# One PSUM ring, merged score halves and DMA transposes in a windowed-attention plus SwiGLU kernel

## The chip, the cores and the metric

The kernel runs on one core of one Trainium2 chip. The metric is the device time of one execution in microseconds (us). Executions are repeated in rounds beside the kernel before on the same chip; e1 to e4, e5 to e8 and e9 to e11 below ran on three different chips, so between these groups the ratios and the traces are compared, not the medians. Engines are named as in the profile: PE (matmuls), PEld (weight loads, which overlap PE: 249.1 and 133.4 us busy in a span of 272.5 before the change), DVE (vector), ACT (scalar), POOL (GpSimd, which also issues the input loads) and SP (which issues outputs and, after the change, transposes). The profile infers from semaphore events who waited for whom.

## The reference, cut to what matters

```python
# q, k, v: (4 batches, 8 heads, 768 positions, 64), float32; n_sink 4, window 128
scores = q @ k.T / 8                      # kept: the first 4 keys, and the last 128 positions
a = softmax(where(keep, scores, -1e9)) @ v
x = a as (3072 tokens, 512)
xn = x / sqrt(mean(x * x) + 1e-6) * rms_g
out = (silu(xn @ w_gate) * (xn @ w_val)) @ w_out      # 512 -> 1536 -> 512
```

The 3072 tokens are 24 blocks of 128 (g = 0 to 23, six to a batch; t is the place in the batch). The feed-forward part (FFN) takes them in six groups of four blocks (G = 0 to 5): gate and value matmuls (pg, pvl), then output matmuls (po).

## The kernel before

The order of PE's instructions is written by hand: the FFN is a list of parts of four to eight matmuls, and the attention of later blocks is woven in between. The attention of a block is a step of four quarters ("slots"). The order on DVE, ACT and POOL is the scheduler's.

```python
def step(g):                                  # before
    slots[0].append(lambda: unit_s(g, 0))     # scores + exponential + mask, half 0 of the heads
    slots[2].append(lambda: unit_s(g, 1))     # half 1
    ...                                       # sink keys (t == 1), sink scores (t in 2, 4)
    slots[1].append(lambda: unit_av(g - 1, 0))   # attention value of the block BEFORE
    slots[3].append(lambda: unit_av(g - 1, 1))
    slots[0].append(lambda: unit_x(g - 3))       # PE transposes of x, copied to xnt by ACT
    slots[2 if t != 5 else 1].append(lambda: unit_t(g + 2))   # PE transposes of q, k; qkT copied by ACT

def unit_sink(b):                             # keys of the four sinks, block-diagonal
    ks = sink.tile([P, HP * KSW], BF16, name="ksk")           # pool "sink" has 2 buffers
    nc.vector.memset(ks, 0.0)
    for hi in range(2):
        nc.vector.tensor_copy(out=ksv[pr, :, ...], in_=QKT[b][pr, 1, :, 0:NS])   # reads qkT of t = 0
```

Names of tiles in the profile: pqk, qkT are the transposed q and k in PSUM and after the copy; pT the scores, et their masked exponentials, ksk the sink keys, pss, esk the sink scores and their exponentials; pv the attention value, x the attention output, sq its squares, xr the normalized x; pxt, xnt its transpose in PSUM and after the copy; hT the product that enters po.

In any step the attention value uses scores of the step before, and x is transposed two steps after that. PSUM is split by use: 4 banks for everything that is one bank wide, 2 for score tiles (pT), 2 for the attention value (pv).

The softmax here doesn't subtract the row's maximum and nothing guards it: scores larger than these inputs give would overflow.

## Time and profile before

Median 275.3 us at the prediction (273.4 to 275.5, three runs), 274.4 us with a fourth run.

From the page of the kernel before, the busy us of each engine (share of the span, instructions), and the busy tenths of the DMA engines in 40 slices of the span:

```profile
PE 249.1 (91%) x1864; PEld 133.4 (49%) x1864; DVE 186.6 (68%) x493; ACT 156.3 (57%) x297; POOL 96.4 (35%) x129
...
DMA  9999999999999930120000220000130000210012
```

The table of windows of the same kernel. The columns are bounds and length in us, then busy us with instructions for PE, PEld, DVE, ACT and POOL, the granted PE clock, the time of the DMA packets as a multiple of the 16 engines' time (packets overlap, so it can exceed 1) and GB/s:

```profile
60.00:80.00 20.00, 18.72 (x180) 10.49 (x178) 16.88 (x58) 18.46 (x36) 19.19 (x22) 1.00 2.40 167
80.00:100.00 20.00, 20.00 (x159) 10.16 (x158) 18.42 (x51) 13.42 (x27) 11.42 (x14) 1.00 1.90 140
120.00:140.00 20.00, 19.93 (x158) 10.04 (x157) 14.92 (x38) 13.65 (x27) 4.29 (x8) 1.00 0.04 15
```

PE is the limit from 60 us on. Until about 95 us the DMA engines are full (9 tenths busy or more in each of the first 14 slices; loads of q, k, v in small pieces: 75440 of the run's 84230 packets are under 512 bytes). What a matmul costs PE is read here from when the next one starts, not from its listed length: the four of pg below are listed with 1.03 us, and the next matmul starts 0.86 us after the first of them, at 132.78 us. Timeline of PE in the kernel before (start, length, what, how many):

```profile
130.18 1.03 PE L417 MATMUL pvl<-xnt,wv 128*128 128x512 bf16 x4
131.14 0.39 PE L279 MATMUL pT<-qkT 64*128 64x256 bf16 x4
131.46 0.40 PE L201 MATMUL pqk<-ident,qs 128*128 128x128 bf16 x4
131.70 0.39 PE L201 MATMUL pqk<-ident,ks 128*128 128x128 bf16 x4
131.92 1.03 PE L417 MATMUL pg<-xnt,wg 128*128 128x512 bf16 x4
```

Four 512-column matmuls take 4 x 216 = 0.864 us, yet pT starts 0.96 us after pvl: entering the scores cost about 0.095 us. The four score matmuls (64 rows each) start in pairs, the two of a pair 3 ns apart; where eight stand in a row (the changed kernel at 64.10 us) a pair starts every 109 ns, so four are worth 4 x 54.5 ns = 0.22 us. Yet 0.32 us pass before pqk: leaving cost 0.10 us. The eight 128-column transposes from 131.46 to 131.92 take 56 ns each from start to start, and are listed with 0.22 to 0.23 us. So this trace puts a round trip into the scores and back at about 0.2 us; why it takes that is not shown.

### The profile page before, as it was taken

What the parts mean: (1) busy time and instruction counts of PE and PEld (TensorE: products, weight loads), DVE (VectorE), ACT (ScalarE), POOL (GpSimd) and SP (SyncE); (2) the same over time, 40 slices, a digit from 0 to 9 for tenths busy, and PEclk for the clock granted to TensorE, in tenths of its full rate; (3) what the DMA queues carried; (4) which work ended last, traced back from release to release, by engine and by line L of the source; (5) the groups of instructions that cost most, each with busy time, mean ns of one, the idle gap of its engine ahead of it and who ended that gap; (6) DMA issues with size and microseconds to landing.
All of it is one profiled execution on the core that took longest, in us unless ns stands there. A gap on an engine that the chain in (4) does not pass through costs nothing.

```text
span 272.5 us, 4924 instructions
## 1 busy us (share of the span) xinstructions
PE 249.1 (91%) x1864; PEld 133.4 (49%) x1864; DVE 186.6 (68%) x493; ACT 156.3 (57%) x297; POOL 96.4 (35%) x129
## 2 busy tenths in 40 slices
PE   1637978998999999999999999899999999999994
PEld 1325766874554544455444454444544454444441
DVE  2591888799788999437798458698337997078710
ACT  2554847769887666557557557558556353333311
POOL 8996369199997601223112001112322000000000
PEclk9999999999999999999999999999999999999998
DMA  9999999999999930120000220000130000210012
GB/s 58 132 175 186 203 160 182 167 155 149 174 199 183 155 14 0 70 88 0 2 1 2 77 77 2 0 2 0 43 113 2 0 2 19 96 41 0 0 68 86
DMA packets 84230, 21.01 MB, mean 77 GB/s; under 512 B 75440, under 2 KB 81072, under 8 KB 84208
## 3 DMA queue, kind: packets, MB, share of 16 engines
q0 software_dynamic: 80752, 14.42, 67.7%
q1 hardware_dynamic: 3456, 6.29, 6.2%
q8 instruction: 14, 0.23, 0.3%
q14 instruction: 8, 0.07, 0.1%
HBM read 28.57 MB, written 6.29 MB: 128 GB/s over the span
## 4 chain that ended last, share of the span: by engine, by line
PE 70%; DVE 8%; DMA 8%; POOL 6%; ACT 5%; issue 1%; POOLq 0%; ACTq 0%; DVEq 0%
PE po L458 22%; PE pg L417 18%; PE pvl L417 18%; DMA ks<-in_k_dram 5%; PE pT L279 4%; DMA wg<-in_moe_w_gate_dram 3%; PE pqk L201 3%; ACT et L286 2%; PE pxt L399 2%; DVE hT L443 2%; POOL ks L90 2%; PE pv L333 1%; ACT qkT L225 1%; POOL qs L90 1%; POOL v_98 L103 1%
## 5 line engine op out<-in xcount | busy, mean ns | idle before, releaser
L417 PE MATMUL pg<-xnt,wg 128*128 128x512 bf16 (+1 forms) x336 | 74.9, 352 | 2.9 <-ACT xnt L403 1.5
L417 PE MATMUL pvl<-xnt,wv 128*128 128x512 bf16 (+1 forms) x336 | 74.1, 349 | 0.0
L458 PE MATMUL po<-wo,hT 128*128 128x512 bf16 x288 | 66.8, 379 | 0.0
L430 ACT ACTIVATE th<-pg 128x512 bf16<-128x512 f32 x72 | 42.8, 595 | 37.8 <-PE pg L417 37.6
L286 ACT ACTIVATE et<-pT 128x1024 bf16<-128x1024 f32 (+1 forms) x48 | 45.2, 946 | 8.9 <-PE pT L279 8.8
L301 POOL TENSOR_SCALAR_AFFINE_SELECT et<-et 128x512 bf16<-128x512 bf16 x20 | 13.2, 660 | 99.6 <-ACT et L286 99.6
L417 PEld LDWEIGHTS <-wg 128*128 128x128 bf16 x336 | 31.3, 99 | 28.1 <-issue 3.1
L417 PEld LDWEIGHTS <-wv 128*128 128x128 bf16 x336 | 31.2, 98 | 25.4 <-issue 0.6
L458 PEld LDWEIGHTS <-hT 128*128 128x128 bf16 x288 | 26.7, 98 | 27.6
L465 ACT ACTIVATE osb<-po 128x512 f32<-128x512 f32 x24 | 14.4, 598 | 24.4 <-PE po L458 19.0
L90 POOL DMA_DIRECT2D ks<-in_k_dram x24 | 21.6, 901 | 6.9 <-DMA wo<-in_moe_w_out_dram 3.5
L225 ACT COPY qkT<-pqk 128x1024 bf16<-128x1024 bf16 x21 | 21.2, 1007 | 5.1 <-PE pqk L201 5.1
L90 POOL DMA_DIRECT2D qs<-in_q_dram x24 | 21.7, 904 | 6.6 <-DMA wo<-in_moe_w_out_dram 2.6
L342 DVE RECIPROCAL rden<-pv 128x4 f32<-128x4 f32 x48 | 8.5, 176 | 19.6 <-PE pv L333 19.5
L279 PE MATMUL pT<-qkT 64*128 64x256 bf16 (+1 forms) x192 | 18.9, 276 | 2.5 <-ACT qkT L225 1.7
L299 DVE TENSOR_TENSOR et<-et,masks 128x1024 bf16<-128x1024 bf16 (+1 forms) x28 | 18.1, 647 | 1.4 <-ACT et L286 1.1
L201 PE MATMUL pqk<-ident,qs 128*128 128x128 bf16 x96 | 10.3, 236 | 7.1 <-DMA qs<-in_q_dram 6.9
L403 ACT COPY xnt<-pxt 128x512 bf16<-128x512 bf16 x24 | 14.0, 581 | 4.6 <-PE pxt L399 4.5
L279 PEld LDWEIGHTS <-qkT 64*128 64x128 bf16 x192 | 6.2, 95 | 18.5 <-issue 17.9
L333 PEld LDWEIGHTS <-et 128*128 128x128 bf16 x192 | 13.5, 100 | 3.2 <-DVE et L299 1.2
L328 PEld LDWEIGHTS <-et 128*128 128x128 bf16 x160 | 12.9, 99 | 3.8 <-DVE x_319 L343 0.7
L399 PE MATMUL pxt<-ident,xr 128*128 128x128 bf16 x96 | 9.9, 229 | 4.2 <-DVE r L374 2.6
(303 smaller groups left out, 341.7 us busy)
## 6 DMA issues: line engine op xcount, KB each, us to landing
out_dram<-osb SPq DMA_DIRECT2D x24, 256.0 KB, 2.0
qs<-in_q_dram POOLq DMA_DIRECT2D x24, 128.0 KB, 7.0
ks<-in_k_dram POOLq DMA_DIRECT2D x24, 128.0 KB, 6.7
wg<-in_moe_w_gate_dram POOLq DMA_DIRECT2D x4, 384.0 KB, 10.0
wv<-in_moe_w_val_dram POOLq DMA_DIRECT2D x4, 384.0 KB, 11.2
wo<-in_moe_w_out_dram POOLq DMA_DIRECT2D x2, 768.0 KB, 11.0
v_98<-in_v_dram POOLq DMA_DIRECT2D x6, 128.0 KB, 7.9
v_100<-in_v_dram POOLq DMA_DIRECT2D x6, 128.0 KB, 7.6
```

Of the source, the lines that this page charges most:

```text
L90: nc.gpsimd.dma_start(out=tl, in_=src[b, :, t * P:(t + 1) * P, :].rearrange("h t d -> t h d"),)
L201: nc.tensor.transpose(out=ps[:, c0 + hp * P:c0 + (hp + 1) * P], in_=src[:, 2 * hp:2 * hp + 2, :], identity=ident,)
L225: nc.scalar.copy(out=QKT[b].rearrange("p i h s -> p (i h) s")[:, :, t * P:(t + 1) * P], in_=ps.rearrange("p (x c) -> p x c", c=P),)
L279: nc.tensor.matmul(out=pT[:, hi, j * 256:j * 256 + w], lhsT=QKT[b][pr, 1, hp, t * P:(t + 1) * P], rhs=QKT[b][pr, 0, hp, t * P:t * P + w], ...
L286: nc.scalar.activation(out=et[:, :, 0:nq, :].rearrange("p x n c -> p x (n c)"), in_=pT.rearrange("p i (j c) -> p (i j) c", c=256)[:, :, 0: ...
L299: nc.vector.tensor_tensor(out=ev, in0=ev, in1=mv, op=ALU.mult)
L333: nc.tensor.matmul(out=dest, lhsT=E[(g, u)][:, x, 0, :], rhs=V16[b][:, t, h, :], start=(t == 0), stop=True, skip_group_check=True,)
L399: nc.tensor.transpose(out=ps[:, kt * P:(kt + 1) * P], in_=xr[:, kt * P:(kt + 1) * P], identity=ident,)
L417: nc.tensor.matmul(out=ps[:, i * n:(i + 1) * n], lhsT=w_sb[:, kt, ft * P:(ft + 1) * P], rhs=XNT[G][:, kt, cols], start=(kt == 0), stop=(kt ...
L430: nc.scalar.activation(out=st["th"], in_=st["pg"], func=ACT.Tanh, scale=0.5)
L458: nc.tensor.matmul(out=st["po"], lhsT=HT[(G, ft // 2)][:, ft % 2, tb * P:(tb + 1) * P], rhs=wo[:, ft, :], start=(ft == 0), stop=(ft == FTN ...
L465: nc.scalar.mul(osb, st["po"], 0.5)
```

## The change

It makes PSUM one ring of eight single banks, runs both score halves of a block back to back, puts a block's attention value into the same step as its scores, moves late transposes from PE to DMA (x from block 8, q and k from block 12), shortens the reciprocal square root by one DVE instruction, and broadcasts the RMS weight by an f32 matmul in place of a broadcast load. It also rearranges the order by hand of the first blocks, which the cut leaves out. Cut to its core:

```diff
-    POOL_MASK_FROM = 2            # by batch
-    MANUAL = {mybir.EngineType.PE}
+    POOL_MASK_FROM = 12           # by block: the same blocks
+    X_DMA_FROM = 8
+    QK_DMA_FROM = 12
+    MANUAL = {mybir.EngineType.PE, mybir.EngineType.SP}
+    ring = ctx.enter_context(tc.tile_pool(name="ring", bufs=8, space=bass.MemoryType.PSUM))
+    def unit_gb():
+        nc.tensor.matmul(out=ps, lhsT=ones, rhs=grow, start=True, stop=True)     # f32
+    def unit_td(g):
+        for i, src in ((1, KS_.pop(g)), (0, QS.pop(g))):
+            nc.sync.dma_start_transpose(out=qkT[:, i, :, t * P:(t + 1) * P], in_=...)
...   # unit_s: both halves, one exponential a bank; unit_av: both halves, one Square a block
     def step(g):
-            slots[0].append(lambda: unit_s(g, 0))
-            slots[2].append(lambda: unit_s(g, 1))
+            slots[0].append(lambda: unit_s(g))
+            slots[2].append(lambda: unit_av(g))
-            slots[1].append(lambda: unit_av(g - 1, 0))
-            slots[3].append(lambda: unit_av(g - 1, 1))
-            slots[0].append(lambda: unit_x(g - 3))
+        if g - 2 < X_DMA_FROM:
+            slots[0].append(lambda: unit_x(g - 2))
+        if X_DMA_FROM <= g < NB:
+            slots[3].append(lambda: unit_x(g))
-            slots[2 if t != 5 else 1].append(lambda: unit_t(g + 2))
+        if g + 2 < QK_DMA_FROM:
+            slots[3 if t != 5 else 1].append(lambda: unit_t(g + 2))
+        if QK_DMA_FROM <= g + 4 < NB:
+            slots[1].append(lambda: unit_td(g + 4))
...   # one pass of sink scores for four blocks from batch 2 on
     with tc.manual_schedule(engines=MANUAL):
         unit_t1(0, 0)
         unit_t1(0, 1)
+        unit_gb()
         unit_t1(1, 0)
```

## The prediction

> **What bounds it.** The page gives PE 91% of the 272.5 us span, DVE 68%, ACT 57%. From 60 us on the table of windows shows PE at 19-20 us of every 20, at full clock. Start-to-start times of matmuls in the timeline: 216 ns for 512 columns, 109 ns for 256, 56 ns for a 128-column transpose, 30 ns for an attention-value matmul, 54 ns for a score matmul of 256 columns (pairs overlap). Summed: about 231 us. The other 41 us: 5 before the first matmul, 17 of gaps up to 30 us (loads, then the rsqrt chain), 5 from 30 to 60 us, 11 after 60 us, 4 of tail. Of the 11 about 8 are switches: some 95 ns to enter and 100 ns to leave each run of 64-row score matmuls.
>
> **What goes.** (1) PE transposes: x from block 8 (16 x 4), q, k from block 12 (12 x 8): 160 x 56 ns = 9.0 us, all where PE limits. (2) Score halves in one run: 24 fewer switches of 0.2 us, 4.8 us, of which I count 3.8 where PE limits. (3) One sink-score pass for two, no gb broadcast on the POOL queue, the 1.5 us gap at 170 us: about 1 us. ACT loses 16 x 0.58 (xnt), 12 x 1.01 (qkT), about 0.45 per block for the Square; it gains 48 fixed parts of about 0.17 us, the exponential being split by bank (585 ns for 512 columns, 1018 for 1024). DVE loses one 0.2 us operation per block. ACT and DVE aren't the limit after 100 us.
>
> **What it adds.** (a) Scores and their attention-value product stand in the same step. The chain is four exponentials (2.4 us) plus mask (0.69 on DVE, about 1.25 per half on POOL). Late, four FFN parts (3.46 us) lie between; I count 1 us. In the first output stage (60-75 us) only 1 to 1.5 us lie between, and the next scores wait for a 1.0 us qkT copy: I estimate a step of 6 us against 4.7 in the trace, three steps, 3.5 us lost. (b) The f32 gb matmul[...] stands ahead of the q1 transposes in the ramp; with longer exponentials I estimate 1 us. (c) 40 DMA transposes of 128 KB. [...] q, k are issued three steps (about 25 us) ahead of use, x about two; even 3 us each should hide.
>
> **Sum.** 9 + 3.8 + 1 - 1 - 3.5 - 1 = 8.3 us off. The constants look tuned, so my penalties may be too high: I add 2.5 us. 275.3 - 10.8 = 264.5 us; 8 in 10 within 258 to 271. Chances: faster by over 2% 0.80, within 0.17, slower 0.03.
>
> **What would show it.** PE instructions 1864 to about 1680; no xnt or qkT copies on ACT after about 100 us; one entry to pT per block; late stages shorter by about 2 us per four blocks. (a): waits of pv for et, by DVE in 60-75 us, by POOL later. (b): first pg later than 21.9 us. (c): no wait of pg for xnt, or of pT for qkT, on a DMA.
>
> **What would make it wrong.** DMA transposes of several us each, serial on one queue and starving the loads (DMA engines over 90% busy to 95 us); the eight-bank ring making pg wait for an old score bank whose exponential queues on ACT; the same-step chain stalling PE in every block (1 us each would cancel the gain); or the early stall not appearing.

Two passages are cut where marked. The 3 us of (c) are an assumption, not a reading.

## The result, and the profile after

The changed kernel took 271.36 us (median of four, 270.8 to 272.2) against 274.44 us: a ratio of 0.988, 95% interval 0.984 to 0.992. Ratios here are the mean time of one kernel's fast runs over that of the other's fast runs of the same rounds, so not quite the ratio of the medians quoted.

The prediction, 264.5 us within 258 to 271, was too low. The time lies just above the range, and in the class (within 2%) that had been given 0.17.

Where the time went is seen by cutting both traces at the same points of PE's work. The table is worked out from start times in the timelines of the two profiled runs (us):

| stage | before | after | difference |
|---|---|---|---|
| start to first gate matmul (ramp) | 21.93 | 23.22 | +1.3 |
| first gate matmul to first po of G 0 | 38.41 | 39.62 | +1.2 |
| first po of G 0 to first gate matmul of G 1 | 20.02 | 28.73 | **+8.7** |
| first gate matmul of G 1 to last matmul | 188.12 | 173.70 | **-14.4** |
| last matmul to the end | 4.02 | 4.45 | +0.4 |
| span | 272.5 | 269.7 | -2.8 |

One caution on these traces. At the first gate matmul PE still runs at half its clock in every one of them (256-column matmuls start 216 ns apart, later 109 ns). The clock records packed with the traces tell when it became full, and this differs: at 25 to 27 us in the kernel before, e2, e5, e7, e9 and e10 (25.4, 26.9, 26.4, 26.4, 25.7, 25.0), at 30 to 32 us in after, e1, e3, e4, e6, e8 and e11 (31.1, 31.2, 31.2, 32.0, 30.6, 30.0, 30.5). The column of the granted clock in the tables of windows reads 1.00 there all the same, since it counts nothing before the first record. The timelines of after and then of e2, which has the same PE work in this stage:

```profile
28.01 1.89 PE L438 MATMUL pvl<-xnt,wv 128*128 128x256 bf16 x8
...
27.57 1.05 PE L438 MATMUL pvl<-xnt,wv 128*128 128x256 bf16 x8
```

The stage from the first gate matmul to the first po took 39.62 us in after and 38.01 in e2, so the late clock is worth about 1.6 us, and more than covers the +1.2 of the table. What decides when it comes is not shown. Runs of one kernel seem to take both: in e1, e6 and e8, profiled with the late clock, the profiled run belongs to a slower group of the fast runs (e1: 267.2 and 267.7 us against 265.6 and 265.7), and in e2, e7, e9 and e10, profiled with the early clock, to the faster. So where two traces differ in this, 1.6 us of their difference are not counted as the edit's.

The late stages gained a little more than the 12.8 us that the prediction's terms amount to there (9 + 3.8 + 1 - 1); part of it, about 0.6 us, is work that the change moved to earlier stages. One early stage, the output matmuls of group 0, gave back more than half. The page of the changed kernel shows PE's share fall, and a dip in the clock granted to PE (tenths, in 40 slices):

```profile
PE 240.3 (89%) x1698; PEld 128.5 (48%) x1698; DVE 179.0 (66%) x471; ACT 135.5 (50%) x267; POOL 96.9 (36%) x128
...
PEclk9999999999997999999999999999999999999999
```

The table of windows of the changed kernel places the loss:

```profile
60.00:80.00 20.00, 13.89 (x141) 8.55 (x139) 13.41 (x42) 11.54 (x24) 17.87 (x21) 1.00 2.53 153
80.00:100.00 20.00, 17.47 (x130) 9.38 (x130) 14.11 (x42) 13.38 (x28) 10.51 (x12) 0.91 2.04 171
120.00:140.00 20.00, 20.00 (x134) 9.64 (x132) 12.02 (x35) 10.74 (x21) 5.25 (x8) 1.00 0.44 102
```

From 60 to 80 us PE fell from 18.7 to 13.9 busy us, and DVE and ACT fell with it. All compute engines idling more at once suggests that they wait for one another or for a DMA, not that one has more to do. In the next window the clock was 0.91. The list of waits of the changed kernel (who waited for whom: us in all, times, longest), PE's from 60 to 95 us, DVE's over the span:

```profile
PE pT L303 <- ACT qkT L237: 5.6, 4, 4.2
PE pv L361 <- DVE et L325: 1.9, 3, 0.9
PE pv L345 <- ACT esk L285: 1.1, 1, 1.1
...
DVE ksk L256 <- DMA qkT<-ks: 3.6, 1, 3.6
```

The last line had not been foreseen at all. Timeline of the changed kernel from 70 to 82 us (in brackets, the idle time before and what ended it):

```profile
70.59 1.37 SPq L245 DMA_TRANSPOSE qkT<-ks  x1
...
76.16 0.39 PE L218 MATMUL pqk<-ident,ks 128*128 128x128 bf16 x4
...
76.38 1.03 PE L482 MATMUL po<-wo,hT 128*128 128x512 bf16 x4
...
78.31 0.35 DVE L256 COPY ksk<-qkT 64x16 bf16<-64x16 bf16 x2 [3.64 <-DMA qkT<-ks]
78.69 0.18 DVE L368 RECIPROCAL rden<-pv 128x4 f32<-128x4 f32 x1
...
79.97 0.63 ACT L376 ACTIVATE sq<-x 128x512 bf16<-128x512 bf16 x1 [3.24 <-DVE x L369]
...
80.60 0.99 ACT L237 COPY qkT<-pqk 128x1024 bf16<-128x1024 bf16 x1
...
81.64 0.61 PE L303 MATMUL pT<-qkT 64*128 64x256 bf16 x8 [4.23 <-ACT qkT L237]
...
82.49 1.91 PE L482 MATMUL po<-wo,hT 128*128 128x512 bf16 x4
```

Read it from the bottom. PE waits 4.2 us for a qkT copy on ACT, though the last transposes that it copies started at 76.2 us and took 0.4 us. ACT has a Square ahead of that copy, and the Square waits 3.2 us for x from DVE. DVE has two tiny copies, 0.17 us each, ahead of the reciprocal for x. They build the sink keys of batch 2, which are first needed at block 14, several steps later. The scheduler put them here, at block 8, and they wait for the DMA transpose of block 12, issued at 70.6 us and landed at 78.3 us. The last line shows the after-effect: four output matmuls took 1.91 us from the first start to the end, where 76.38 us shows 1.03. They started 427 ns apart in place of 216, so PE was at half its clock until about 85.7 us (the clock record: 3.4 us from 82.3 us on). PE had hardly a gap in it, so by estimate half of it, 1.7 us, was lost on top of the wait.

Two things are read from the traces here. DVE did not run the reciprocal ahead of the two copies: the attention-value matmuls before it had ended by 75.2 us, but it started at 78.69, after the copies and the 3.6 us of idle time before them. And a gap of 4.2 us on PE (to 81.6 us) was followed by the half clock from 82.3 us on; in e4 the half clock came with a gap of 2.3 us (64.2 to 66.5 us, half clock from 66.1 to 69.5), while gaps of 1.2 to 1.9 us in the kernel before, e4, e6 and e11 were not followed by it. The traces show no more than that of what takes the clock down.

The DMA transposes themselves, in the list of DMA issues of the changed kernel, from 60 to 100 us and then from 120 to 220 us (the last number is the median time from issue to landing, us):

```profile
qkT<-ks SPq DMA_TRANSPOSE x3, 7.7
qkT<-qs SPq DMA_TRANSPOSE x3, 8.2
xnt<-xr SPq DMA_TRANSPOSE x2, 7.2
...
xnt<-xr SPq DMA_TRANSPOSE x11, 2.4
qkT<-ks SPq DMA_TRANSPOSE x7, 2.4
qkT<-qs SPq DMA_TRANSPOSE x7, 2.5
```

The first list is of 60 to 100 us, beside the saturated loads (DMA at 9 tenths or more throughout): there a transpose took 7 to 8 us at the median to land; from 120 to 220 us it took 2.4 to 2.5. The prediction had no measured time for one, and its assumption of 3 us was less than half of what they took beside the loads. 39 of the 40 issues also held SP's queue for 1.2 to 1.4 us, one for 1.9. The list of waits shows none of PE for a DMA transpose, since PE's first readers come later. What had been overlooked was a reader on DVE.

### The profile page after: what moved, and what is told of

Same layout as the page of the kernel before. It is cut to its first block, busy times and chain, and to the rows that moved or that the text cites. A ratio compares the mean times of both kernels' runs of the same rounds, so it can differ in the third digit from the quotient of the medians.

```text
span 269.7 us, 4662 instructions
## 1 busy us (share of the span) xinstructions
PE 240.3 (89%) x1698; PEld 128.5 (48%) x1698; DVE 179.0 (66%) x471; ACT 135.5 (50%) x267; POOL 96.9 (36%) x128
## 4 chain that ended last, share of the span: by engine, by line
PE 80%; DVE 7%; ACT 6%; DMA 4%; issue 1%; POOL 0%; ACTq 0%; POOLq 0%
PE pg L438 22%; PE pvl L438 22%; PE po L482 21%; PE pT L303 5%; DMA qkT<-ks 3%; PE pv L361 2%; PE pqk L218 2%; DVE et L325 2%; ACT qkT L237 2%; DMA ks<-in_k_dram 2%; PE pv L356 2%; PE pv L345 1%; DVE x L369 1%; PE pss L279 1%; ACT et L312 1%
## 5 line engine op out<-in xcount | busy, mean ns | idle before, releaser
L459 DVE SCALAR_TENSOR_TENSOR p<-th,pg 128x512 bf16<-128x512 bf16 x72 | 49.1, 682 | 32.3 <-ACT th L451 31.8
L312 ACT ACTIVATE et<-pT 128x512 bf16<-128x512 f32 (+1 forms) x96 | 46.4, 568 | 13.1 <-PE pT L303 13.0
L467 DVE TENSOR_TENSOR hT<-p,pvl 128x512 bf16<-128x512 bf16 x72 | 49.3, 685 | 3.4
L488 ACT ACTIVATE osb<-po 128x512 f32<-128x512 f32 x24 | 14.4, 601 | 30.9 <-PE po L482 26.9
L98 POOL DMA_DIRECT2D qs<-in_q_dram x24 | 21.5, 894 | 7.2 <-DMA wo<-in_moe_w_out_dram 2.1
L376 ACT ACTIVATE sq<-x 128x512 bf16<-128x512 bf16 x24 | 15.1, 628 | 16.4 <-DVE x L369 16.4
L303 PE MATMUL pT<-qkT 64*128 64x256 bf16 (+1 forms) x192 | 15.4, 279 | 8.5 <-ACT qkT L237 6.7
L111 POOL DMA_DIRECT2D v<-in_v_dram x24 | 21.3, 888 | 4.4 <-DMA qs<-in_q_dram 1.4
L369 DVE TENSOR_TENSOR x<-pv,rden 128x256 bf16<-128x256 f32 x48 | 19.8, 420 | 0.6
L361 PE MATMUL pv<-v,et 128*128 128x65 bf16 x192 | 17.3, 200 | 3.1 <-DVE et L325 3.1
L404 DVE SCALAR_TENSOR_TENSOR xr<-x,r,gb 128x512 bf16<-128x512 bf16 x24 | 19.1, 798 | 0.6
L303 PEld LDWEIGHTS <-qkT 64*128 64x128 bf16 x192 | 7.9, 96 | 17.9 <-issue 17.2
```

The costliest lines, as they stand in the source:

```text
L98: nc.gpsimd.dma_start(out=tl, in_=src[b, :, t * P:(t + 1) * P, :].rearrange("h t d -> t h d"),)
L111: nc.gpsimd.dma_start(out=V16[b][:, t, :, 0:D], in_=v[b, :, t * P:(t + 1) * P, :].rearrange("h t d -> t h d"),)
L303: nc.tensor.matmul(out=pT[(u, hi)][:, j * 256:j * 256 + w], lhsT=QKT[b][pr, 1, hp, t * P:(t + 1) * P], rhs=QKT[b][pr, 0, hp, t * P:t * P + w],
L312: nc.scalar.activation(out=et[:, 2 * hi:2 * hi + 2, 0:nq, :].rearrange("p x n c -> p x (n c)"), in_=pT[(u, hi)].rearrange("p (j c) -> p j ...
L361: nc.tensor.matmul(out=dest, lhsT=E[(g, u)][:, x, 0, :], rhs=V16[b][:, t, h, :], start=(t == 0), stop=True, skip_group_check=True,)
L369: nc.vector.tensor_tensor(out=x16[:, 4 * u:4 * u + 4, :], in0=pvv[:, :, 0:D], in1=rden.unsqueeze(2).to_broadcast((P, 4, D)), op=ALU.mult,)
```

## The experiments

e1 to e4 are the changed kernel with one edit each. e5 to e10 keep the edit of e1, and e11 is e5 without it. All results were correct. Times are medians; ratios are to the kernel before of the same rounds.

### e1: the hoisted copies kept back

```diff
-        ks = sink.tile([P, HP * KSW], BF16, name="ksk")
+        ks = sink.tile([P, HP * KSW], BF16, name="ksk", bufs=1)
```

With one buffer, the copies of batch 2 need the sink scores of batch 1 to be done, so they cannot be hoisted past block 10.

> The changed kernel with one edit: the block-diagonal sink keys (ksk) get one buffer in place of two, so the copies for batch 2 can't be placed on DVE before block 10's sink scores have been read; they then come long after the q, k transpose of block 12 has landed. Theory A (head of line): in the changed kernel these two copies stand on DVE ahead of block 8's reciprocal and wait 3.6 us for the DMA transpose; DVE, ACT's qkT copy and PE stand still in turn (4.2 us before the scores at 81.6 us) and the clock throttles for a while (matmuls at 427 ns). Expected: no DVE wait of ksk on a DMA, the first output stage 28.7 -> about 22.5 us, 271.4 -> about 265.5 us. Rival B (same-step chain of exponential, mask and attention value sets the length of the steps): the next wait takes over, at most 2 us won. Rival C (the transposes crowd the saturated DMA engines and the loads come late): nothing won.

Measured: 266.43 us, ratio 0.970 (0.965 to 0.975). The wait of ksk for a DMA is gone, the first output stage took 24.94 us in place of 28.73, all later stages stayed as they were (173.69 us), and the mean granted clock is 1.0. The table of windows of e1:

```profile
60.00:80.00 20.00, 15.60 (x158) 9.58 (x156) 14.86 (x48) 14.25 (x29) 18.39 (x22) 1.00 2.20 150
80.00:100.00 20.00, 18.27 (x147) 9.55 (x146) 16.16 (x45) 11.77 (x25) 11.00 (x13) 1.00 1.93 169
```

PE got back about 2.5 us over the two windows and the full clock, but not the 38.7 us of before. Its waits from 60 to 95 us in e1:

```profile
PE pv L361 <- DVE et L325: 2.8, 5, 0.9
PE pT L303 <- ACT qkT L237: 2.3, 4, 0.9
PE pv L345 <- ACT esk L285: 1.1, 1, 1.1
```

Theory A was right about the place, too high about the size: 3.8 us won in this stage where about 6 had been expected. PE's waits in these lists fell only from 8.6 to 6.2 us, as waits for et grew; the other 1.4 us of the gain fit the half clock that no longer came. What is left, 24.9 against 20.0 us before, belongs to something else. So neither theory A nor rival B alone explains the 8.7 us, and rival C (nothing won) is out.

### e2: all transposes back on PE

```diff
-    X_DMA_FROM = 8
-    QK_DMA_FROM = 12
+    X_DMA_FROM = NB
+    QK_DMA_FROM = NB
-            if b < 2 and t in (2, 4):
+            if t in (2, 4):
...   # and the pass of sink scores for four blocks removed
```

> The changed kernel with all transposes back on PE (and two sink-score passes a batch, which the later arrival of q then needs). Theory A: the first output stage falls to about 22.5 us since ksk waits for no DMA, and the later stages get longer by 160 transposes x 56 ns = 9 us: about 274 us in all. Rival B: the first output stage stays at about 28.7 us, about 280 us in all. Rival C: as A. The sum of the stages from the first gate matmul of group 1 on tells what the DMA transposes are worth: 9 us expected.

Measured: 274.77 us, ratio 1.002 (0.997 to 1.007). From the first gate matmul of group 1 to the last matmul it took 182.53 us against 173.70 after: the DMA transposes are worth 8.8 us there, 9.0 expected. (e2 also makes two passes of sink scores in place of one; by the distances between starts read above, eight matmuls of 256 columns, 8 x 109 ns, cost PE what four of 512 do, 4 x 216 ns.) The first output stage took 25.17 us, close to e1's 24.94. So with no DMA transpose at all that stage is still 5 us longer than before: what is left there has nothing to do with DMA transposes. PE's waits from 60 to 95 us are those of e1 to the digit (2.8, 2.3 and 1.1 us).

### e3: the RMS-weight matmul later

```diff
         unit_t1(0, 1)
-        unit_gb()
...
         unit_s(1)
+        unit_gb()
         unit_av(0)
```

> The changed kernel with the f32 matmul that broadcasts the RMS weight moved from before the q1 transposes to after block 1's scores, where PE waits for masks anyway. Theory: it delayed the ramp by 1.3 us (first gate matmul 23.2 us against 21.9 before); expected first gate matmul at about 22.0 us and 271.4 -> about 270.2 us. Rival: the ramp's end is set by the loads and the later chain, the gate matmul comes earlier but the first output matmul stays at 62.8 us: under 0.4 us won.

Measured: 271.45 us median, three fast runs of 269.8, 272.9 and 270.0 us and the profiled one in the slow state; ratio of the fast runs 0.986 (0.979 to 0.993), a verdict of unclear at the 2% line. The trace is that of the slow run, but its low clock lies at 80 to 100 us (0.83), not in the ramp (1.00 to 60 us). The first gate matmul came at 23.45 us, no earlier. The timeline shows why: the q1 transposes did start at 7.3 us in place of 9.05, but the matmul now stood in front of block 0's attention value and held that back, to 15.6 us, and its copy on DVE delayed a mask. The place was badly chosen, so the run says nothing against the theory; e8 tests it again.

### e4: attention value one step later, alone

```diff
-            slots[2].append(lambda: unit_av(g))
+        if 5 < g <= NB:
+            slots[2].append(lambda: unit_av(g - 1))
-        if X_DMA_FROM <= g < NB:
-            slots[3].append(lambda: unit_x(g))
+        if X_DMA_FROM <= g - 1 < NB:
+            slots[3].append(lambda: unit_x(g - 1))
```

> The changed kernel with the attention-value product of each block from 5 on moved to the next step (as before the change), so that a whole step lies between scores and their use; ksk copies stay as they are. Theory A: the waits of attention value for masks and sink exponentials in the first output stage (about 0.9 + 0.7 + 1.3 + 0.8 us) go, the ksk stall stays: 28.7 -> about 25.5 us, in all about 268 us; later stages unchanged within 1 us. Rival B: the stage goes to about 21 us and the total to about 264 us.

Measured: 272.18 us, ratio 0.990 (0.984 to 0.996), the first output stage 30.65 us. Both expectations missed. The edit left PE's transposes of x (block g - 2 in step g) right behind an attention value that had moved to step g - 1. PE's waits from 60 to 98 us show the wait for masks gone and a new one in its place. (Part of the 30.65 is the clock, which was half twice in this stage, for 3.4 us each; its mean was 0.91 from 60 to 80 and from 80 to 100 us. The first time came with the wait of 2.3 us for xr: the four output matmuls from 66.89 us on took 1.91 us.)

```profile
PE pT L303 <- ACT qkT L237: 5.4, 4, 4.0
PE pxt L423 <- DVE xr L404: 4.2, 2, 2.3
```

A stagger must be moved as a whole; one link alone moves the wait.

### e5: the whole stagger put back

On e1: attention value one step after its scores (as in e4), and x on PE one step later as well.

```diff
-        if g - 2 < X_DMA_FROM:
-            slots[0].append(lambda: unit_x(g - 2))
+        if g - 3 < X_DMA_FROM:
+            slots[0].append(lambda: unit_x(g - 3))
```

> The one-buffer kernel (ksk fixed, 266.4 us) with the stagger of the kernel before put back from block 5 on: attention value one step after its scores, PE transposes of x two steps after (in the run that moved attention value alone, x followed it at once and PE waited for xr instead). Score halves stay merged. Theory A2 (what is left of the first output stage, 24.9 us against 20.0 before, is the chain within a step): the waits of attention value for masks go, the stage falls to about 21.5 us and the total to about 263 us. Rival B2 (ACT's own work and the order qkT copy, exponentials, scores set the step): the stage stays within 1 us of 24.9.

Measured: 260.36 us, ratio 0.950 (0.946 to 0.953). The first output stage took 19.87 us, as short as before the change (20.02), and the stage ahead of it 36.98 us against e1's 39.67. The table of windows of e5:

```profile
60.00:80.00 20.00, 18.34 (x176) 10.83 (x174) 15.91 (x55) 18.20 (x37) 15.81 (x19) 1.00 2.27 160
80.00:100.00 20.00, 20.00 (x149) 10.05 (x148) 19.08 (x48) 10.94 (x24) 11.88 (x14) 1.00 1.99 165
```

Of PE's waits from 60 to 95 us only this is left in e5:

```profile
PE pT L303 <- ACT qkT L237: 1.7, 4, 0.8
```

PE is back at 18.3 and 20.0 us, and the waits for et and esk are gone. The rest of the loss in this stage was the chain of exponential, mask, attention value and x within one step, in which the qkT copy stands too (e6). The stage fell further than theory A2 expected (21.5 us), and rival B2 is out as stated.

The single stages must be compared with care, since the edit also moves some work across their borders. From the first gate matmul to the last matmul of all e5 took 231.25 us and e1 238.30, a difference of 7.1 us. But e1's trace has the late clock and e5's the early one: 1.6 us of the 7.1, all in the stage ahead, where by the count of PE's instructions another 0.5 us is work moved into the next stage. So the stagger is worth about 5.4 us, nearly all in the first output stage. The ratios, 0.970 and 0.950 of about 274.5 us, say about 5.5, each known to 1 to 1.4 us.

### e6 and e7: q, k transposes earlier in the step

```diff
-            slots[3 if t != 5 else 1].append(lambda: unit_t(g + 2))
+            slots[1].append(lambda: unit_t(g + 2))
```

e6 makes this edit on e1, e7 on e5.

> The one-buffer kernel with only the PE transposes of q and k moved from the last quarter of a step to its second quarter, so that the ACT copy of qkT doesn't stand right before the next scores. Theory A2: the 3.4 us that the scores wait for the qkT copy (all over the early stages) go, masks are still waited for; the first output stage 24.9 -> about 23 us, total about 264.5 us. Rival B2: the stage goes to about 21 us.

> Both edits together. Theory A2 and B2 both give the stage about 20 us, as PE's own work in it then sets its length, and about 261.5 us in all; if it stays above 23 us, neither is the cause and PE's clock or the DMA loads have to be looked at.

Measured: e6 262.45 us, ratio 0.958 (0.954 to 0.962), first output stage 21.70 us; e7 260.09 us, ratio 0.949 (0.946 to 0.953), first output stage 19.34 us. e6 lies between its two expectations: with the copy out of the way, PE's waits from 60 to 90 us were 1.8 us for et and 0.6 us for esk. So in e1 the place of the qkT copy was a good part of the loss, and the stagger covers it too: on top of e5 the edit brings only 0.5 us in that stage. The two edits don't add, as they take slack from the same step.

### e8: the RMS-weight matmul first

```diff
+        unit_gb()
         unit_t1(0, 0)
         unit_t1(0, 1)
-        unit_gb()
```

On e1, where PE waits for the first q until 4.8 us anyway.

> The one-buffer kernel with the f32 RMS-weight matmul put before the first transposes, where PE waits for the first q anyway (its input is a 2 KB transfer issued at 0.8 us). Theory: that matmul (2.0 us) held back the q1 transposes by 1.6 us; first gate matmul 23.2 -> about 22.2 us and total about 265.4 us. Rival: the stage after the ramp takes the gain back (it ends at 62.9 us whatever the ramp does), under 0.4 us in all.

Measured: 265.87 us, ratio 0.969 (0.963 to 0.974); e1 in other rounds had 0.970, an overlap, so the times don't settle it. The traces do for the ramp: first gate matmul at 22.55 us against e1's 23.19, and the span 0.85 us shorter. The matmul ran from 2.6 to 4.6 us and delayed no transpose. Of the 0.85 us, 0.2 fit the clock, which was full at 30.0 us here and at 31.2 in e1.

### e9: the score halves apart again

On e5, for blocks from 5 on:

```diff
-            slots[0].append(lambda: unit_s(g))
+            slots[0].append(lambda: unit_s(g, (0,)))
+            slots[1].append(lambda: unit_s(g, (1,)))
```

> The staggered kernel (one ksk buffer, attention value a step later; 260.4 us) with the two score halves of each block from 5 on apart again, in the first and second quarter of a step. Theory: each further run of 64-row score matmuls costs PE about 0.2 us (0.095 to enter, 0.105 to leave), so 19 blocks x 0.2 = 3.8 us: about 264 us, and the stages from the first gate matmul of group 1 on about 2.8 us longer in sum. Rival: the merge is worth nothing by itself (under 1 us), the later stages got shorter through the ring alone.

Measured: 264.31 us, ratio 0.962 (0.958 to 0.966), against e5's 260.36 and 0.950. From the first gate matmul of group 1 to the last matmul 177.17 us against 174.39, 2.8 us longer, as expected. Both traces have the early clock. Merging the halves is worth that by itself: 14 blocks are left in these stages, so about 0.2 us per further entry into 64-row matmuls holds.

### e10 and e7 once more: the best version

e10 is e7 with `unit_gb()` first, run in five rounds beside e7.

> The kernel with stagger, one ksk buffer and early q, k transposes (260.1 us) with the RMS-weight matmul put first as well. The same move gave 0.6 us at the first gate matmul and 0.85 us at the end in the one-buffer kernel's trace; expected 259.3 us, 0.5 to 1 us under the same kernel without it. Rival: nothing, the gain stays in the ramp.

> The kernel of e7_stagger_qk_early once more, as the partner of e10_gb_first_too on the same chip: 260.1 us expected.

Measured on the same chip: e10 259.29 us, ratio 0.944 (0.941 to 0.947); e7 260.59 us, ratio 0.948 (0.944 to 0.951). The difference is 1.3 us between the medians and 0.8 us between the traces (257.2 and 258.0 us); the intervals overlap, so the gain of this last edit is likely and small. The traces, both with the early clock, are the better measure: the first gate matmul came at 22.12 against 22.96 us. e10 beats both kernels, by 5.6% the one before.

### e11: the stagger, with two buffers for ksk

e5 with the edit of e1 taken out.

> The staggered kernel with ksk's two buffers back, so that the copies that wait for the DMA transpose stand early on DVE again. Theory (two separate causes that add): the DVE wait on the transpose is back (3 to 4 us) and the total rises from 260.4 to about 264 to 266 us. Rival (with a step of slack the late DVE no longer reaches PE): under 1 us.

Measured: 264.33 us, ratio 0.961 (0.958 to 0.964) against e5's 0.950 (0.946 to 0.953) on another chip; the traces are 3.7 us apart. The wait is back, in the list of waits from 70 to 85 us:

```profile
DVE ksk L256 <- DMA qkT<-ks: 3.0, 1, 3.0
```

So the two causes stand each on its own. In the traces 2.3 of the 3.7 us between e5 and e11 are in the first output stage (22.21 against 19.87): that is the price of the wait when PE has a step of slack and the clock stays full. The other 1.4 us are in the stage ahead (38.36 against 36.98), before the wait: there PE's starts drift apart by about that much from 27.3 to 30.5 us, since e11's trace has the late clock and e5's the early one. So the total that was expected came out partly by luck; the ksk copies are worth 2.3 us of the rise.

## Why the prediction was wrong

**Right: what bounds the kernel and what is saved.** PE limits after 60 us, and what was costed by start-to-start times came out as costed: the DMA transposes 8.8 us (e2 against after) where 9.0 had been predicted, the merged halves 2.8 us after the first gate matmul of group 1 (e9 against e5), 3.8 us having been counted wherever PE limits. PE's instructions fell to 1698 (about 1680 predicted). The two measured gains make 11.6 of the 14.4 us; 1.5 us more are the gap near 170 us that is gone (below), and the rest was not separated, nor were the ring, the exponential by bank and the shorter reciprocal square root tested alone. The late same-step stalls, 1 us in the sum, didn't show: after 120 us no two starts on PE were over 0.45 us apart. Nor did the ring of eight banks hold up a gate matmul; the one such wait of before (1.5 us near 170 us, pg for DVE) is gone.

**Right: the ramp.** 1 us was predicted for the matmul ahead of the q1 transposes and the longer exponentials; the ramp grew by 1.3 us, and e8 traces 0.6 us of it to the matmul's place (e10 against e7: 0.8). The rest, the longer exponentials among it, was not tested alone.

**Wrong: the size of term (a), "a step of 6 us against 4.7 in the trace, three steps, 3.5 us lost".** The mechanism was real, the foreseen waits of pv for et and of pT for qkT, and its size was off. e1 has no ksk wait any more. The first score matmuls of its blocks 7 to 10 start at 64.12, 71.04, 78.31 and 85.08 us, steps of 6.9, 7.3 and 6.8; before they start at 61.92, 66.70, 72.47 and 77.30, steps of 4.8, 5.8 and 4.8. That is 5.6 us more in three steps. By stages it is 4.9 us (24.94 against 20.02), and putting the stagger back takes 5.1 us off this stage and about 5.4 in all (e5 against e1, without the 1.6 us of the clock). So the chain within a step cost about one and a half times what had been counted. The sum in the prediction held the exponentials, the mask and the qkT copy; in e1's timeline from 71.0 to 78.3 us three more stand on ACT in the same round: the xnt copy (0.6 us) and the sink exponential (0.4) ahead of the attention value, and the square (0.8) ahead of the qkT copy.

**Wrong: the step "even 3 us each should hide" in term (c).** For PE it held. But the argument took only PE for a reader of the transposed keys. The ksk copies on DVE read them too, and the scheduler, which orders DVE, had put them at block 8, five blocks ahead of their use in program order (they are issued in step 13). There they waited on a transpose that took 7.7 us from issue to landing, and DVE, then ACT, then PE stood still behind them. That cost 3.8 us in e1's comparison, the half clock after the gap included, and 2.3 us where there was slack (e11). "What would make it wrong" had named transposes of several us each, but as a queue that starves the loads; e1 left the loads as they were and won its 3.8 us.

**Wrong: the last adjustment.** The terms summed to 8.3 us off. 2.5 us were then added since the constants looked tuned. That was no reading of the profile. Without it the forecast would have been 267.0 us, 4.4 us from the measured 271.4 in place of 6.9.

## What to carry to other kernels

When a producer is moved from an engine to a DMA queue, list every reader of its output on every engine, and look where each stands in the order of its engine: here two 0.17 us copies that stood too early held up DVE, and ACT and PE behind it, for what was left of the landing time (3.6 us of 7.7). A stagger between scores, their use and the next transpose is worth keeping when halves are merged: here the merge and the DMA transposes gave 11.6 us in the late stages, the lost stagger and one hoisted copy took about 9 us of it back, and both could be had (259.3 us against 274 to 275). And before two single traces are subtracted, it pays to look whether both came to full clock at the same place: here that alone was 1.6 us.
